# Strided V in two loads a batch, and a new list schedule, in a sparse-attention and gated-projection kernel on one core

## The chip, the core and the metric

The kernel runs on one core of one Trainium2 chip. Its engines work from queues of their own: TensorE (PE, with its weight loads shown apart as PEld), VectorE (DVE), ScalarE (ACT), GpSimd (POOL) and SyncE (SP), which here only issues DMAs. The metric is the device time of one execution, in microseconds (us), lower being better. The span of a profiled execution is the time from its first to its last instruction.

## The reference

Eight batches, eight heads, 576 positions, head size 64. The first four heads see a local window of 32 positions; the other four see the positions with the same residue modulo 32. The attention output then passes a causal convolution of five taps with a sigmoid, and two 512x512 products. All inputs are float32, except that the three weights arrive as float64.

```python
scores = scale * np.matmul(q, k.transpose(0, 1, 3, 2))
mask_local = (rel >= 0) & (rel < stride)
mask_strided = (rel >= 0) & (pos[None, :] % stride == pos[:, None] % stride)
...
attn = np.exp(scores - max) / (sum + 1e-09)
x = np.matmul(attn, v)                 # heads side by side: (8, 576, 512)
...
gate = 1.0 / (1.0 + np.exp(-gate_pre)) # gate_pre: five taps of x
val = x @ w_val
out = gate * val @ w_out
```

## The kernel before, in words

The work of a batch falls into groups, each with a name of a letter, the batch and a number; this text writes L, S, Y, T, V, P and C for the kinds.

- L: scores of the local heads, three groups a batch of 24 matmuls `bank<-KL,qLs`. DVE adds a mask and takes the maximum, POOL subtracts, ACT takes the exponential, POOL scales, DVE transposes. Y: the product with V, two groups a batch of 40 matmuls `bank<-PL,vLs`.
- S: scores of the strided heads, two groups a batch of 32 matmuls `bank<-KBS,qSs`, with the same softmax. T: the product with V, two groups a batch of 16 matmuls `bank<-BDS,vSs`. T reads all 128 partitions of `vSs`.
- C: the convolution of the first of four channel blocks of batch 0 on PE, 10 matmuls `bank<-xs,gate` and `bank<-xs,diag`; all other convolutions are on DVE and ACT (`taps`).
- V and P: the two products by 512x512 weights, in 48 and 36 groups of 12 matmuls. To keep float32 accuracy, the operands are split into a high and a low part (`xhi`, `xlo`, `ghi`, `glo`), and so are the weights (`wv`, `wo`), which are made from float64 at the start, through the buffers `xs`, `osb` and `gate`.
- Filler: matmuls of zeros, `bank<-idle`, that the planner puts into gaps on PE in the first 75 us of its own time, so that PE stays busy. They are fixed in number and place when the program is built; PE runs them whether or not the data that they wait for has come.

One buffer each serves `qLs`, `KL`, `qSs`, `KBS`, `vLs` and `vSs` for all batches, so that the load for a batch can be issued only when the last matmul of the batch before has read it. All loads and stores are issued by SP, in one order, through eight completion semaphores in turn: the ninth DMA is issued when the first has landed, and so on.

The order on every engine comes from `Plan.issue`, a list scheduler that runs when the program is built (lines 133 to 234). It keeps a clock for each engine, and takes of the steps that can start at the earliest time the one whose group has the lowest number in the table `RANK`. Its model of a load is `ISSUE` on SP, then a common pipe that the loads fill one after another for as long as each takes (the `took` that the function `load` sets), then `TO_END` until the data may be read. Its model of PE's program is that it is fetched in blocks of `BLOCK` = 256 words: when PE enters a block, the fetch of the next one starts and takes `FETCH` (more while loads are under way), and PE cannot enter that one before it is there. A matmul of float32 operands counts 4 words, for two passes of a weight load and a matmul; one of bf16 or of the split operands counts 2. The first block begins with 66 words already used.

```python
199                    there = at_edge + self.FETCH + min(2.0, 0.5 * max(0.0, pipe - at_edge))
...
203                free[engine] = start + self.ISSUE
204                pipe = max(pipe, start + self.TO_DATA) + took
205                done = pipe + self.TO_END
```

A row of PE's order is one matmul of this program; the profile counts a float32 one twice (72 rows of L are `x144` there).

Of the kernel before, what the change touches and what calls it, by code (L numbers as in the profile page):

```python
# [19 lines left out]
NT = 18  # L20
# [3 lines left out]
P = 128  # L24
# [9 lines left out]
class Bank:  # L34
# [12 lines left out]
    def now(self):  # L47
        ap = self.hold["tile"]
        for name, a, k in self.chain:
            ap = getattr(ap, name)(*a, **k)  # L50
        return ap
# [6 lines left out]
class Plan:  # L58
# [11 lines left out]
    ENGINES = ("pe", "dve", "act", "pool", "sp")  # L70
    WINDOW, QUIET, BUSY, SLOW = 3.413, 0.48, 0.85, 1.9

    BLOCK, FETCH = 256, 2.4
    ISSUE, TO_DATA, TO_END = 0.6, 1.2, 0.65

    def __init__(self):
        self.filler, self.banks, self.holds = None, None, []
# [160 lines left out]
def tile_sparse_attention_moe(  # L238
# [13 lines left out]
    nc = tc.nc  # L252
# [6 lines left out]
    plan = Plan()  # L259

    def tiles(n, shape, name, dtype=F32, space=None):
        return [(space or pool).tile(shape, dtype, name=f"{name}{i}") for i in range(n)]
# [10 lines left out]
    def size(ap):  # L273
        n = 1
        for _, k in list(now(ap).ap)[1:]:
            n *= k
        return n
# [21 lines left out]
        return (T.matmul, dict(out=out, lhsT=lhsT, rhs=rhs, start=first, stop=last))  # L299

    def load(group, out, in_):
        n = out.ap[0][1] * size(out)
        plan.add("sp", max(n * 4 / 320e3 + (0.25 if group[-1] == "0" or "w" in group else 0.08), 0.45), group, [(nc.sync.dma_start, dict(out=out, in_=in_))])


    ident = pool.tile([P, P], F32, name="ident")
# [12 lines left out]
    vSs = pool.tile([P, 8, 256], F32, name="vSs")  # L319
# [11 lines left out]
    gates = tiles(4, [P, 2 * S], "gate")  # L331
    BDS = Ring(tiles(NB, [P, 16, 4, NT], "BDS"))
    PS = Ring(tiles(1, [P, 32, 32], "PS"))
# [84 lines left out]
    def weight_part(name, src, dst, e, raw, t, u):  # L418
        raw = raw.rearrange("p (c f) -> p c f", c=4).bitcast(U32)
        load("load " + name, raw, src.bitcast(U32)[:, 2 * P * e:2 * P * (e + 1)].rearrange("(c p) f -> p c f", p=P))  # L420
        cols = slice(P * e, P * (e + 1))
        from_f64("make " + name, raw.rearrange("p c (f w) -> p (c f) w", w=2), t, u, dst[0][:, :, cols], dst[1][:, :, cols])
# [30 lines left out]
    def load_qk(b, kind):  # L453
        group = f"load q{kind}{b}"
        if kind == "L":
            load(group, qLs[:, :, :], qL[b])
            load(group, KL[:, :, STRIDE:], kL[b])
            return

        for j in range(2):  # L460
            load(group, qSs[j::2, :2 * S], qS[b, 64 * j:64 * j + 64])
        for j in range(2):
            load(group, KBS[j::2, j, :, :], kS[b, 64 * j:64 * j + 64])

    def load_v(b, kind):
        group = f"load v{kind}{b}"
        if kind == "L":

            for a in range(2):
                for p in range(2):  # L470
                    at = slice(64 * a + 32 * p, 64 * a + 32 * p + 32)
                    load(group, vLs[at, 1 - a:], vL[b].rearrange("(w r) f -> r w f", r=32)[:, 8 * a:9 * a + 9, 2 * D * p:2 * D * p + 2 * D])
        else:
            for g in range(4):
                load(group, vSs[32 * g:32 * g + 32:2], vS[b, g, 0:16])
            for g in range(4):
                load(group, vSs[32 * g + 1:32 * g + 32:16], vS[b, g, 16:NT])

    def attend_local(b):
        xs = xss[b % 2]  # L480
# [200 lines left out]
    for b in range(B):  # L681
        load_qk(b, "L")
        load_v(b, "L")
        load_qk(b, "S")
        load_v(b, "S")
        attend_local(b)
        attend_strided(b)
        if b == 0:

            raw = [osb2.rearrange("p i f -> p (i f)"), raws[2], raws[3], osb2.rearrange("p i f -> p (i f)")]  # L690
            for e in range(4):
                weight_part(f"wo{e}", w_out, wo, e, raw[e], *[gates[2 * i + e % 2][:, S:S + DM] for i in range(2)])
            zero("dve", "zero xs1", xss[1][:, :, 0:PADK])
        gate(b)
        for k in ((3 * b // 2,) if b % 2 == 0 else (3 * (b // 2) + 1, 3 * (b // 2) + 2)):
            value(k)
            project(k)
    names = list(dict.fromkeys(s[2] for s in plan.steps))
    tile_sparse_attention_moe.end = plan.issue(dict(zip(names, RANK)))


NB = 1
NPL = 1
TAKEN = set()
# [4 lines left out]
CONV = {(0, 0)}  # L709
HELD = set()  # L710
RANK = [
# [12 lines left out]
]  # L724


# [39 lines left out]
```

## Time and profile before

| what | value |
|---|---|
| runs | 331.25, 336.93 and 336.55 us, median 336.55 us |
| the profiled execution | 331.2 us, of which the span is 329.4 us |
| busy in the span: DVE | 225.4 us (68%) |
| busy in the span: ACT, POOL | 189.8 us (58%), 180.8 us (55%) |
| the chain that ended last, by engine | PE 82%, DMA 10%, issue 3%, SP's queue 2% |
| `bank<-idle` on PE | 117 recorded, 30.5 us busy |
| read from and written to HBM | 32.79 MB and 9.44 MB |

A row of the timeline gives the start and the length in us, the engine, the line, the operation, the tile written and those read, the shapes, and the number of instructions joined in the row; in brackets stand the idle time of the engine just before and what ended it. "issue" there means that the engine waited for nothing that the profile shows. Nearly all records have line 226, where the planner issues the instruction; line 351 is the filler. The page's lines by time have 40 slices, 8.235 us each.

### The profile page before, as it was taken

The numbers are of one execution on the slowest core, as the hardware profiler recorded it, in microseconds if no ns is written. First come the engines' busy times: TensorE is split into PE (matmuls) and PEld (weight loads), VectorE is DVE, ScalarE is ACT, GpSimd is POOL, SyncE is SP. The second block draws the span as 40 slices with busy tenths as digits, with TensorE's granted clock in tenths as the row PEclk, the third lists the DMA queues.
The fourth block names the chain that finished last, engine by engine and source line by source line (L and its number), as shares of the span: only waits on it lengthen the run. The fifth ranks groups of instructions, "written<-read, shape, count | busy, mean of one in ns | idle before, by whom it ended". The sixth has DMA issues, their size and how long they took to land.

```text
span 329.4 us, 11806 instructions
## 1 busy us (share of the span) xinstructions
PE 311.0 (94%) x5113; PEld 261.2 (79%) x5120; DVE 225.4 (68%) x438; ACT 189.8 (58%) x373; POOL 180.8 (55%) x213
## 2 busy tenths in 40 slices
PE   8986999997999999899999998999999989999995
PEld 3545567787889989688998887988998978999884
DVE  4479399997988989698592288876776951764300
ACT  4036675695578746574753294498369748442421
POOL 9664767978653964674384276556067722502610
PEclk9997699999999999999999999999999998999999
DMA  7999944469314452676302476036202200100022
GB/s 236 252 178 329 271 137 154 148 203 258 107 66 146 149 211 100 207 235 176 105 2 84 142 197 211 2 105 175 73 1 66 103 4 32 66 32 32 34 96 96
DMA packets 27267, 42.98 MB, mean 130 GB/s; under 512 B 3088, under 2 KB 16912, under 8 KB 26640
## 3 DMA queue, kind: packets, MB, share of 16 engines
q1 hardware_dynamic: 27216, 42.24, 42.9%
q8 instruction: 40, 0.66, 0.9%
q14 instruction: 11, 0.09, 0.1%
HBM read 32.79 MB, written 9.44 MB: 128 GB/s over the span
## 4 chain that ended last, share of the span: by engine, by line
PE 82%; DMA 10%; issue 3%; SPq 2%; ACT 0%; DVE 0%
PE bank L226 73%; PE bank L351 9%; DMA qSs<-in_qS_dram 6%; DMA vSs<-in_vS_dram 3%; SPq L226 2%; DMA vLs<-in_vL_dram 1%; ACT osb L226 0%; DVE idle L350 0%; DVE none L354 0%
## 5 line engine op out<-in xcount | busy, mean ns | idle before, releaser
L226 DVE SCALAR_TENSOR_TENSOR taps<-xs,cw,taps 128x576 f32<-128x576 f32 x124 | 100.6, 811 | 14.3 <-ACT taps L226 12.5
L226 PE MATMUL bank<-xhi,wv 128*128 128x384 f32 x384 | 99.7, 340 | 0.0
L226 PE MATMUL bank<-wo,ghi 128*128 128x512 f32 x288 | 90.8, 397 | 0.0
L226 POOL TENSOR_TENSOR glo<-GV,ghi 128x384 fp32r<-128x384 f32 x48 | 48.3, 1013 | 63.4 <-ACT ghi L226 62.1
L226 PEld LDWEIGHTS bank<-xhi,wv 128*128 128x128 f32 x384 | 68.8, 188 | 2.2
L226 PE MATMUL bank<-xlo,wv 128*128 128x384 f32 x192 | 64.5, 336 | 0.0
L226 PEld LDWEIGHTS bank<-wo,ghi 128*128 128x128 f32 x288 | 53.6, 190 | 11.2
L226 POOL TENSOR_TENSOR xlo<-xs,xhi 128x576 fp32r<-128x576 f32 x32 | 46.2, 1451 | 19.9 <-ACT xhi L226 19.8
L226 PE MATMUL bank<-wo,glo 128*128 128x512 f32 x144 | 56.5, 393 | 0.0
L226 DVE SCALAR_TENSOR_TENSOR GV<-gate,bank 128x384 f32<-128x384 f32 x48 | 26.0, 547 | 34.1 <-PE bank L226 18.0
L226 ACT ACTIVATE osb<-bank 128x512 f32<-128x512 f32 x36 | 21.2, 596 | 30.0 <-PE bank L226 24.5
L226 ACT COPY xs<-bank 128x288 f32<-128x288 f32 x64 | 32.0, 548 | 8.3 <-PE bank L226 8.1
L226 ACT CAST ghi<-GV 128x384 fp32r<-128x384 f32 x48 | 24.0, 510 | 21.6 <-DVE GV L226 21.4
L226 PEld LDWEIGHTS bank<-xlo,wv 128*128 128x128 f32 x192 | 36.0, 188 | 0.0
L351 PE MATMUL bank<-idle 128*128 128x512 bf16 x117 | 30.5, 411 | 5.2 <-issue 3.8
L226 ACT ACTIVATE gate<-taps 128x576 f32<-128x576 f32 x31 | 20.4, 658 | 24.7 <-DVE taps L226 24.6
L226 ACT COPY BDS<-PT 32x288 f32<-32x288 f32 x64 | 27.7, 433 | 9.7 <-DVE PT L226 8.9
L226 PEld LDWEIGHTS bank<-wo,glo 128*128 128x128 f32 x144 | 27.2, 189 | 5.9
L226 POOL TENSOR_TENSOR SML<-SML,ST 128x384 f32<-128x384 f32 x24 | 20.3, 845 | 19.0 <-DVE ST L226 18.8
L351 PEld LDWEIGHTS <-idle 128*128 128x128 bf16 x124 | 12.2, 103 | 20.6 <-issue 7.8
L226 DVE TENSOR_REDUCE ST<-SML 128x6 f32<-128x384 f32 (+1 forms) x48 | 26.0, 545 | 0.9 <-ACT SML L226 0.5
L226 PEld LDWEIGHTS bank<-PL,vLs 32*64 32x64 f32 x1280 | 21.9, 143 | 5.8 <-issue 3.4
(69 smaller groups left out, 371.1 us busy)
## 6 DMA issues: line engine op xcount, KB each, us to landing
out_dram<-osb SPq DMA_DIRECT2D x36, 256.0 KB
qSs<-in_qS_dram SPq DMA_DIRECT2D x16, 288.0 KB
qLs<-in_qL_dram SPq DMA_DIRECT2D x8, 576.0 KB
KL<-in_kL_dram SPq DMA_DIRECT2D x8, 576.0 KB
KBS<-in_kS_dram SPq DMA_DIRECT2D x16, 288.0 KB
vSs<-in_vS_dram SPq DMA_DIRECT2D x32, 128.0 KB
vLs<-in_vL_dram SPq DMA_DIRECT2D x16, 160.0 KB
vLs<-in_vL_dram SPq DMA_DIRECT2D x16, 144.0 KB
```

Source lines behind the costliest of these rows:

```text
L226: got = [fn(**{k: now(x) for k, x in kw.items()}) for fn, kw in calls]
L351: plan.filler = lambda at: T.matmul(out=at, lhsT=idle[:, :P], rhs=idle[:, :], start=True, stop=True)
```

## The change

Three things change in the source. The strided V of a batch is loaded by two DMAs, one of 64 partitions (keys 0 to 15 of each of four groups) and one of 8 partitions (keys 16 and 17), where it was four of 16 partitions and four of 2. The planner's numbers change: `FETCH` from 2.4 to 3.0, `TO_END` from 0.65 to 1.2, and what a load adds to its bytes becomes 0.2 for every load, where it was 0.25 for batch 0 and the weights and 0.08 for the rest. And the table `RANK` is another one. No instruction on DVE, ACT or POOL is added or taken away.

```diff
-    BLOCK, FETCH = 256, 2.4
-    ISSUE, TO_DATA, TO_END = 0.6, 1.2, 0.65
+    BLOCK, FETCH = 256, 3.0
+    ISSUE, TO_DATA, TO_END = 0.6, 1.2, 1.2
...
     def load(group, out, in_):
-        n = out.ap[0][1] * size(out)
-        plan.add("sp", max(n * 4 / 320e3 + (0.25 if group[-1] == "0" or "w" in group else 0.08), 0.45), group, [(nc.sync.dma_start, dict(out=out, in_=in_))])
+        n = 1
+        for k in out.shape:
+            n *= k
+        plan.add("sp", max(n * 4 / 320e3 + LOAD, 0.45), group, [(nc.sync.dma_start, dict(out=out, in_=in_))])
...
-            for g in range(4):
-                load(group, vSs[32 * g:32 * g + 32:2], vS[b, g, 0:16])
-            for g in range(4):
-                load(group, vSs[32 * g + 1:32 * g + 32:16], vS[b, g, 16:NT])
+            for rows, keys in ((slice(0, P, 2), slice(0, 16)), (slice(1, P, 16), slice(16, NT))):
+                load(group, vSs[rows].rearrange("r n f -> r (n f)"),
+                     vS[b, :, keys].rearrange("g t n f -> g t (n f)"))
...
+LOAD = 0.2
...
 RANK = [
-    223, 130, 85, 82, 100, 54, 253, 247, 56, 131, 268, 93, 53, 134, 241, 140, 277, 144, 154, 271, 136, 147, 195, 58,
+    84, 243, 209, 155, 196, 173, 29, 32, 256, 79, 135, 208, 6, 194, 267, 25, 234, 221, 158, 21, 42, 145, 232, 11,
...
```

What this does to the order is seen best on SP, whose queue PE waits for. The first place is the start of the program, SP's first rows before. `in_w_val` and `in_w_out` are parts of the two weights, `in_conv_w` the taps.

```order
L226 DMA xs_77<-in_w_val_dram 128x4x256
L226 DMA qSs<-in_qS_dram 64x1152
L226 DMA osb_110<-in_w_out_dram 128x4x256
L226 DMA qLs<-in_qL_dram 128x1152
L226 DMA KL<-in_kL_dram 128x2x576
L226 DMA vSs<-in_vS_dram 16x2048 x2
L226 DMA KBS<-in_kS_dram 64x1152 x2
L226 DMA qSs<-in_qS_dram 64x1152
L226 DMA vSs<-in_vS_dram 16x2048 x2
L226 DMA xs_78<-in_w_val_dram 128x4x256
```

The same rows of SP now:

```order
L226 DMA xs_77<-in_w_val_dram 128x4x256
L226 DMA qSs<-in_qS_dram 64x1152
L226 DMA osb_110<-in_w_out_dram 128x4x256
L226 DMA cw_91<-in_conv_w_dram 128x4x10
L226 DMA qLs<-in_qL_dram 128x1152
L226 DMA KBS<-in_kS_dram 64x1152
L226 DMA KL<-in_kL_dram 128x2x576
L226 DMA KBS<-in_kS_dram 64x1152
L226 DMA xs_78<-in_w_val_dram 128x4x256
L226 DMA qSs<-in_qS_dram 64x1152
```

The taps and half of the strided K now stand ahead of the local K (`KL`), and V of the strided heads has moved behind them.

A little further on SP now stand the local loads of batches 1 and 2 and what lies between them, whose place in the stream the prediction uses:

```order
L226 DMA vSs<-in_vS_dram 64x1x2048
L226 DMA qLs<-in_qL_dram 128x1152
L226 DMA KL<-in_kL_dram 128x2x576
L226 DMA xs_78<-in_w_out_dram 128x4x256
L226 DMA qSs<-in_qS_dram 64x1152
L226 DMA KBS<-in_kS_dram 64x1152 x2
L226 DMA vSs<-in_vS_dram 8x1x2048
L226 DMA xs_78<-in_w_out_dram 128x4x256
L226 DMA qSs<-in_qS_dram 64x1152
L226 DMA osb_110<-in_w_out_dram 128x4x256
L226 DMA qLs<-in_qL_dram 128x1152
L226 DMA KL<-in_kL_dram 128x2x576
```

Between the local loads of batch 1 and those of batch 2 stand seven rows, among them the three parts of `w_out` that were still to come. Ahead of the first of these rows stand, besides the ten above, the four loads of `vLs` (32x9x128 twice and 32x10x128 twice) and one more part of `w_val` each into `xs_78` and `xs_77`.

The second place is the loads of the strided heads of batch 3, some 70 us into the run before. SP before:

```order
L226 DMA vLs<-in_vL_dram 32x10x128
L226 DMA qSs<-in_qS_dram 64x1152
L226 DMA KBS<-in_kS_dram 64x1152 x2
L226 DMA qSs<-in_qS_dram 64x1152
L226 DMA vSs<-in_vS_dram 16x2048
L226 DMA qLs<-in_qL_dram 128x1152
L226 DMA KL<-in_kL_dram 128x2x576
L226 DMA vSs<-in_vS_dram 16x2048 x3
L226 DMA vSs<-in_vS_dram 2x2048
```

SP now, at the loads for the same batch:

```order
L226 DMA vLs<-in_vL_dram 32x10x128
L226 DMA vSs<-in_vS_dram 64x1x2048
L226 DMA qSs<-in_qS_dram 64x1152
L226 DMA KBS<-in_kS_dram 64x1152 x2
L226 DMA vSs<-in_vS_dram 8x1x2048
L226 DMA qLs<-in_qL_dram 128x1152
L226 DMA qSs<-in_qS_dram 64x1152
L226 DMA KL<-in_kL_dram 128x2x576
```

Five issues of V around these loads have become two, and one part of Q now stands behind the local Q.

PE has the same matmuls in another order, with 122 fillers where it had 124. Its order up to the first V group, in groups with the number of rows, is:

| | rows of PE's order, up to the first V group |
|---|---|
| before | filler 51, L 72, filler 18, S 64, filler 12, Y 80, filler 8, C 5, L 24, C 5, L 24, T 16, L 24, filler 21, T 16, filler 1, S 64, filler 12, V |
| now | filler 59, L 72, filler 14, S 64, filler 47, L 72, T 16, Y 40, S 64, L 24, T 16, Y 40, L 24, filler 1, C 10, T 16, V |

By then L has 48 rows and T 16 rows more than before; the other kinds have as many.

The rows of PE between the last S group of one batch and the first of the next, which is the time that the loads of `qSs` and `KBS` have, are before at the least: for batch 3 two V groups, a T and an L; for batch 6 (the next shortest) a V group, a Y, an L and a P. Now they are at the least, for batch 4: two P groups, a V, a Y and a T.

22 rows, old and new, of the table RANK are left out of this document.

## The prediction

> **What bounds the kernel now.** I read the page first (busy shares, the 40 slices), then PE's timeline, then the waits and SP's timeline.
>
> ```profile
> PE 311.0 (94%) x5113; PEld 261.2 (79%) x5120; DVE 225.4 (68%) x438; ACT 189.8 (58%) x373; POOL 180.8 (55%) x213
> ...
> GB/s 236 252 178 329 271 137 154 148 203 258 107 66 146 149 211 100 207 235 176 105 2 84 142 197 211 2 105 175 73 1 66 103 4 32 66 32 32 34 96 96
> ...
> q8 instruction: 40, 0.66, 0.9%
> ...
> L351 PE MATMUL bank<-idle 128*128 128x512 bf16 x117 | 30.5, 411 | 5.2 <-issue 3.8 <-DVE none L354 1.2
> ```
>
> PE is the bound: no other engine is above 68%. Of its 311 us, 30.5 us are filler, so 280.5 us are work that this change does not touch, and some 49 us of the 329.4 us span can move. Nearly all of that lies before the first V group:
>
> ```profile
> 1.19 12.76 PE L351 MATMUL bank<-idle 128*128 128x512 bf16 x50 [1.19 <-DVE none L354]
> 13.88 1.72 PE L226 MATMUL bank<-KL,qLs 64*32 64x64 f32 x144
> 15.54 4.06 PE L351 MATMUL bank<-idle 128*128 128x512 bf16 x17
> 19.52 0.29 PE L226 MATMUL bank<-KBS,qSs 128*32 128x36 f32 x9
> 20.83 1.26 PE L226 MATMUL bank<-KBS,qSs 128*32 128x36 f32 x119 [1.02 <-issue]
> 22.02 2.12 PE L351 MATMUL bank<-idle 128*128 128x512 bf16 x8
> 27.58 0.82 PE L351 MATMUL bank<-idle 128*128 128x512 bf16 x3 [3.44 <-issue]
> 28.33 3.28 PE L226 MATMUL bank<-PL,vLs 32*64 32x64 f32 x124
> 31.95 1.33 PE L226 MATMUL bank<-PL,vLs 32*64 32x32 f32 x36 [0.34 <-issue]
> 33.62 3.19 PE L351 MATMUL bank<-idle 128*128 128x512 bf16 x7 [0.34 <-issue]
> ...
> 55.83 0.70 PE L226 MATMUL bank<-xhi,wv 128*128 128x384 f32 x2
> ```
>
> The "issue" gaps are edges of instruction blocks. PE and PEld together have 10,233 instructions in 40 fetched blocks, so about 256 to a block. Counted from the 66 words at the start, word 512 falls in the sixth S row of PE's order, where the gap of 1.02 us stands (after 9 profiled matmuls, two to a row), and word 768 some ten fillers later, where the 3.44 us stand. Word 256 passed in the 23rd L row, at about 14.4; the block behind word 512 came at 20.83, so its fetch took 6.4 us. The next took 20.83 to 27.58, 6.75 us; the third, to the gap at 31.95, 4.4 us.
>
> The rest of the recoverable time is in eight later gaps:
>
> ```profile
> 66.44 0.33 PE L226 MATMUL bank<-KBS,qSs 128*32 128x36 f32 x15 [1.27 <-issue]
> 77.00 1.33 PE L226 MATMUL bank<-KBS,qSs 128*32 128x36 f32 x128 [1.96 <-DMA qSs<-in_qS_dram]
> 138.94 1.33 PE L226 MATMUL bank<-KBS,qSs 128*32 128x36 f32 x128 [1.40 <-DMA qSs<-in_qS_dram]
> 195.63 1.39 PE L226 MATMUL bank<-PL,vLs 32*64 32x64 f32 x78 [0.23 <-DMA vLs<-in_vL_dram]
> 199.35 0.31 PE L226 MATMUL bank<-KL,qLs 64*32 64x64 f32 x7 [1.24 <-issue]
> 224.07 0.46 PE L226 MATMUL bank<-PL,vLs 32*64 32x64 f32 x15 [0.34 <-issue]
> 269.94 0.27 PE L226 MATMUL bank<-PL,vLs 32*64 32x64 f32 x2 [1.00 <-issue]
> 270.39 1.97 PE L226 MATMUL bank<-BDS,vSs 128*64 128x72 f32 x32 [0.18 <-issue]
> ```
>
> They sum to 7.6 us: 3.6 us waits for loads, 4.0 us block edges. Where a block holds little work, PE reaches its end before the next is there.
>
> **The change part by part.** *V in two loads.* SP's rows for four old loads, and the wait that its rows show:
>
> ```profile
> SPq L226 <- DMA KL<-in_kL_dram: 7.0, 4, 2.6
> ...
> 13.08 0.37 SPq L226 DMA_DIRECT2D xs<-in_w_val_dram  x1
> ...
> 51.82 2.50 SPq L226 DMA_DIRECT2D vSs<-in_vS_dram  x4
> ...
> 57.30 2.52 SPq L226 DMA_DIRECT2D vSs<-in_vS_dram  x4
> ```
>
> Eight issues took 5.0 us of SP, about 0.63 us each; two take 1.3 us, 3.7 us a batch less. The bytes are the same, and no PE wait before is for `vSs`, so by itself this is worth nothing on the path. PE's other work hides it; if that cover went, the 3.7 us are what a Q load behind V could gain at one place. On the other side, loads that carry more each leave eight semaphores for more bytes; no row prices that, and I bound it by one issue, 0.6 us. I take 0.
>
> *The later gaps.* Before batch 3's S there are two V groups (2.2 us each), a T and an L (0.7): 6.2 us, and PE waited 1.96 us; before batch 6's a V, a Y (1.4), an L and a P (2.9): 7.2 us, and it waited 1.40. So these loads need 8.2 to 8.6 us from the last reader. The durations of groups are these rows:
>
> ```profile
> 61.85 2.76 PE L226 MATMUL bank<-PL,vLs 32*64 32x64 f32 x160
> ...
> 66.72 1.22 PE L226 MATMUL bank<-BDS,vSs 128*64 128x72 f32 x32
> ...
> 84.83 0.72 PE L226 MATMUL bank<-KL,qLs 64*32 64x64 f32 x48
> 85.48 0.62 PE L226 MATMUL bank<-xhi,wv 128*128 128x384 f32 x2
> ...
> 87.67 0.63 PE L226 MATMUL bank<-wo,ghi 128*128 128x512 f32 x2
> ...
> 90.53 1.22 PE L226 MATMUL bank<-BDS,vSs 128*64 128x72 f32 x32
> ```
>
> (V is 85.48 to 87.67, P 87.67 to 90.53, Y half of 2.76.) The shortest stretch now is two P, a V, a Y and a T, 10.5 us: enough by 2 us. I take the waits for Q as gone. I then walked PE's new order in blocks of 256 words with these durations. After the first V group the shortest blocks before held 1.9, 2.4, 2.7 and 2.8 us of work, and those are the four with gaps; now they hold 3.1, 3.7, 4.1 and 4.1. From the gaps at 224.07 and 269.94 a late fetch takes 2.4+0.34 = 2.8 and 2.7+1.0 = 3.7 us, so at most 0.6 us is left. T at 270.39 also ran in 1.97 instead of 1.22 us, the granted clock being below 1 there: 0.75.
>
> ```profile
> 260.00:280.00 20.00, 18.82 (x285) 16.50 (x284) 9.12 (x15) 12.74 (x25) 6.37 (x8) 0.91 0.11 41
> ```
>
> For new waits that I can't see (SP's order puts stores of P ahead of some loads) I take another 0.6 us, bounds 0 and 3. Together −7.6 −0.75 +1.2 = −7.2 us, bounds −8.4 and −4.8.
>
> *Work moved ahead of the first V.* Two L groups and a T that before came later: 2×0.7+1.2 = 2.6 us off the rest.
>
> *The start.* 59 fillers take 12.76 + 9×0.22 = 14.8, to 15.95. Local K lands about then: behind 2.84 MB, against 2.52 MB before, when SP, which waits there for the semaphore of that load, went on at 13.08. At the slices' 252 GB/s that is 1.3 us later, 14.4. (The memset of `vSs` on POOL, now in the middle of the mask, is covered by these fillers.) L 1.72 and 14 fillers (3.3) bring 21.0. Word 256 now passes at 16.3, its fetch comes 6.4 later at 22.7, and word 512 in the fourth S row is a gap of 1.6. S ends at 24.1, word 768 is the sixth of 47 fillers, at 25.4, and the fetch from 22.7 ends at 29.5 (27.1 by the 4.4 us). The planner lets a fetch run beside fillers, but they stand behind it on PE: 41 are still to run, 9.1 us, to 38.6. Then L, from 38.6 to 40.7; word 1024 at 39.9.
>
> Now come three blocks of 2.7, 1.6 and 2.4 us of work (L, T, Y, S, L, T, all float32). At 4.4, 4.4 and 3.3 us a fetch they end at 44.3, 48.7 and 52.0. The loads allow that: by the slices 10.42 MB are moved at 41.2, and local Q and K of batch 2 end at 11.33 MB, so at 44.5 and, with the 2.5 us that the load at 13.08 took beyond its bytes, at 47.0; they are needed near 49. Left are 36 Y rows (1.25), L, ten C rows (5.7, by the rows below), T and a filler: 9.1, and the first V group starts at 61.
>
> ```profile
> 40.75 2.21 PE L226 MATMUL bank<-xs,gate 128*128 128x288 f32 x8
> ...
> 42.80 0.65 PE L226 MATMUL bank<-xs,diag 128*128 128x288 f32 x2
> ```
>
> With 2.8 us a fetch in these blocks, and the short end of the filler gap, the loads bind instead: L of batch 2 from 47.0, V at about 56. With half a window at half clock it is 64. I take 60 between them, +4.2 us.
>
> **The sum.** 329.4 + 4.2 − 2.6 − 7.2 = 323.8 us of span; the execution took 331.2, 1.8 more, so 325.6 us. The median of the runs, 336.55, is 5.4 above the profiled execution; 325.6 is 1.7% below that execution and 3.3% below the median.
>
> The Trainium skill, "Runtime: NRT & Kernel Launch", "Instruction fetch mechanics", has blocks of 16 KiB or 256 instructions, fetched while the current one runs, and calls the cost of crossing an edge "mostly hidden". The 40 blocks agree; the gaps of 3.44 and 1.02 us at the counted words do not. By that rule the block gaps would be no term, and the sum would go by the second rival.
>
> **The rivals.** *The start runs through* (V at 55 to 56): fetches are short because fewer loads are in flight. 329.4 − 0.3 − 2.6 − 7.2 + 1.8 = 321 us. For it: the 4.4 us fetch at 31.95; against it: two of three were above 6.
>
> *Block counts do not govern the late gaps.* They would reappear, 4.0 us: 329.6 us. For it: the profile says only "issue". Against it: the four shortest blocks are the four with gaps. The page of the skill named above stands for this one.
>
> *The start is lost.* The gap at 25.4 halves the clock, as before:
>
> ```profile
> 20.00:40.00 20.00, 15.00 (x307) 10.09 (x309) 13.74 (x32) 11.40 (x26) 11.11 (x12) 0.74 1.11 269
> ```
>
> A mean of 0.74 is about 10 us at half clock; there 7 fillers took 3.19 instead of 1.55 and Y 4.6 instead of 2.76. In the new order up to 24 fillers would lie in those 10 us, +5 us: 331 to 334 us.
>
> *Slower.* The same gap, but the waits at the three short blocks never leave PE a busy stretch, so that it stays at half clock to the first V: 41 fillers at 0.43 (+8.5) and 17 us of groups at 1.5 times (+8.5), V at 73 where the walk without waits has 56: +17. 329.4 + 17 − 2.6 − 7.2 + 1.8 = 338.4 us, just over 2% above the profiled execution. It decides if the clock is half beyond about 60 us. Against it: before it came back within 10 us. That the edit does nothing is no case; the orders differ everywhere.
>
> **How the numbers follow.** The forecast, 323 to 328 us, 0.38; the start runs through, 0.20; late gaps stay, 0.17; the start is lost, 0.17; slower, 0.08. The range 318 to 333 holds all but the fast end of the second, the upper half of the fourth and the last. Two per cent, about what a measurement of this kernel can tell from no change, is at 324.6 us against the profiled execution and at 329.8 against the median. Counting 0.20, six tenths of 0.38 and a little of the third: faster 0.46; same 0.46; slower 0.08.
>
> **What would show it.** Right: no wait of an S group for `qSs` over 0.5 us; no "issue" gap over 0.6 us after 65 us; a gap of 2 to 4 us among the third run of fillers, and the first V group between 56 and 64. Wrong: late waits for `KL` or `vLs` behind a store on SP, gaps in long blocks, or a granted clock below 0.9 in slices after 65 us.

## The result

The changed kernel takes 352.81 us (median of four runs, 351.7 to 356.94) where the kernel before takes 334.08 (four runs, 331.25 to 336.93; the fourth, 331.6, was not yet among those ahead of the prediction): the ratio is 1.067, 95% interval 1.051 to 1.082. Ratios here compare the means of only those runs of each kernel that lie within 1.5% of its fastest, while medians are of all runs, so that a ratio can differ from the quotient of the medians. The kernel is slower, and the prediction of 325.6 us (318 to 333) with 8 in 100 for slower was wrong. The profiled execution took 353.87 us, its span 352.1.

The page of the changed kernel, the lines that answer to those of before:

```profile
PE 320.2 (91%) x5118; PEld 266.7 (76%) x5118; DVE 227.5 (65%) x438; ACT 189.7 (54%) x373; POOL 182.0 (52%) x213
...
PEclk9998966999599998999789999999999999999999
DMA  7999556129304494247400436414421031002022
...
L353 PE MATMUL bank<-idle 128*128 128x512 bf16 x122 | 31.2, 417 | 4.1 <-issue 2.6
```

The work of each engine is as before. PE is busy for 9 us more, and the granted clock goes with that: in slices of 8.8 us it is below 0.8 from 44 to 62, from 88 to 97 and from 167 to 176 us, where before it was so only from 25 to 41:

```profile
PEclk9997699999999999999999999999999998999999
```

The idle time has grown by some 14 us. The timeline of PE shows where; the rows below, of the changed kernel, are all its gaps over 1 us, and its first V group:

```profile
1.19 14.87 PE L353 MATMUL bank<-idle 128*128 128x512 bf16 x59 [1.19 <-DVE none L356]
22.66 1.29 PE L226 MATMUL bank<-KBS,qSs 128*32 128x36 f32 x123 [1.53 <-issue]
27.77 10.93 PE L353 MATMUL bank<-idle 128*128 128x512 bf16 x42 [2.63 <-issue]
...
43.50 0.60 PE L226 MATMUL bank<-PL,vLs 32*64 32x64 f32 x8 [1.12 <-DVE SML L226]
45.23 1.47 PE L226 MATMUL bank<-PL,vLs 32*64 32x64 f32 x72 [1.13 <-DVE PL L226]
50.15 0.94 PE L226 MATMUL bank<-KBS,qSs 128*32 128x36 f32 x46 [2.00 <-issue]
55.12 1.39 PE L226 MATMUL bank<-PL,vLs 32*64 32x64 f32 x78 [1.23 <-DVE SML L226]
...
67.71 0.62 PE L226 MATMUL bank<-xhi,wv 128*128 128x384 f32 x2
...
91.07 2.19 PE L226 MATMUL bank<-BDS,vSs 128*64 128x72 f32 x32 [5.88 <-DMA vSs<-in_vS_dram]
133.82 0.71 PE L226 MATMUL bank<-KL,qLs 64*32 64x64 f32 x48 [3.24 <-DMA KL<-in_kL_dram]
173.68 2.19 PE L226 MATMUL bank<-BDS,vSs 128*64 128x72 f32 x32 [4.87 <-DMA vSs<-in_vS_dram]
246.14 0.44 PE L226 MATMUL bank<-xhi,wv 128*128 128x384 f32 x1 [1.12 <-issue]
```

The waits for `qSs` and most block gaps of before are gone after 68 us, as forecast, and the gap of 2.63 us among the third run of fillers was forecast too. But three waits of 3 to 6 us for loads have come, two of them for `vSs`, for which PE had no gap before. The T groups behind the two waits for `vSs` run in 2.19 us where 1.22 is usual; from 91.0 to 93.3 us the granted clock is 0.50. And the first V group starts at 67.71, where it started at 55.83 before and was forecast between 56 and 64. The chain of the changed kernel says how long four loads took from their issue to their landing (start, length, what):

```profile
57.45 8.97 DMA vSs<-in_vS_dram
...
78.15 12.79 DMA vSs<-in_vS_dram
...
121.03 12.65 DMA KL<-in_kL_dram
...
163.65 9.94 DMA vSs<-in_vS_dram
```

The load at 78.15 is the one of 8 partitions. Its 64 KB would take 0.5 us at the 122 GB/s that this profile has on average, so its bytes alone do not explain 12.79 us.

### The profile page after: what moved, and what is told of

Same layout as the page of the kernel before. It is cut to its first block, busy times and chain, and to the rows that moved or that the text cites. A ratio compares the mean times of both kernels' runs of the same rounds, so it can differ in the third digit from the quotient of the medians.

```text
span 352.1 us, 11735 instructions
## 1 busy us (share of the span) xinstructions
PE 320.2 (91%) x5118; PEld 266.7 (76%) x5118; DVE 227.5 (65%) x438; ACT 189.7 (54%) x373; POOL 182.0 (52%) x213
## 2 busy tenths in 40 slices
DMA packets 26755, 42.98 MB, mean 122 GB/s; under 512 B 2576, under 2 KB 16400, under 8 KB 26128
## 4 chain that ended last, share of the span: by engine, by line
PE 78%; DMA 13%; DVE 3%; issue 2%; ACT 2%; POOL 1%; SPq 1%; ACTq 0%
PE bank L226 69%; DMA vSs<-in_vS_dram 9%; PE bank L353 9%; DMA KL<-in_kL_dram 4%; DVE gate L226 2%; SPq L226 1%; DVE ST L226 1%; ACT BDS L226 1%; POOL wv L226 0%; DVE SML L226 0%; ACT osb L226 0%; ACT xs L226 0%; POOL SML L226 0%; POOL PB L226 0%; ACT taps L226 0%
## 5 line engine op out<-in xcount | busy, mean ns | idle before, releaser
L226 PE MATMUL bank<-xhi,wv 128*128 128x384 f32 x384 | 104.3, 353 | 1.1 <-issue 1.1
L226 PEld LDWEIGHTS bank<-xhi,wv 128*128 128x128 f32 x384 | 71.5, 196 | 3.5 <-issue 1.4
L226 PE MATMUL bank<-xlo,wv 128*128 128x384 f32 x192 | 66.5, 346 | 0.0
L226 PEld LDWEIGHTS bank<-xlo,wv 128*128 128x128 f32 x192 | 37.5, 195 | 0.0
L226 PE MATMUL bank<-BDS,vSs 128*64 128x72 f32 x512 | 22.0, 245 | 12.0 <-DMA vSs<-in_vS_dram 12.0
L226 PEld LDWEIGHTS bank<-BDS,vSs 128*64 128x64 f32 x512 | 19.7, 151 | 15.6 <-issue 8.5
```

The costliest lines, as they stand in the source:

```text
L226: got = [fn(**{k: now(x) for k, x in kw.items()}) for fn, kw in calls]
```

## The experiments

**Which part costs.** The first four runs cross the two orders with three ways to load V. In all of them the instructions of PE, DVE, ACT and POOL stand in the order of the kernel that is named; only SP's DMAs of `vSs` differ. For eight loads in the new order, one step of the planner issues four DMAs:

```diff
+                def four(out, in_, step=step, keys=keys):
+                    for g in range(4):
+                        nc.sync.dma_start(out=vSs[32 * g + (step > 2):32 * g + 32:step], in_=vS[b, g, keys])
+                load(group, vSs[(step > 2):P:step].rearrange("r n f -> r (n f)"), None, four)
```

> The order of the changed kernel, instruction for instruction on PE, DVE, ACT and POOL, with strided V again in four loads of 16 partitions and four of 2, issued where the two loads stood. Theory A (the merged load runs on few of the DMA engines, because its DRAM side has four groups as its outermost dimension, and holds up what is queued behind it): the waits for vSs (12.0 us) and KL (3.2 us) of the changed kernel go, with some 6 us of half clock behind them: 329 to 336 us, in place of 352.8. Theory B (the new order is what costs, whatever the loads): 345 to 353 us. Theory C (a load that is large as such lands late, and fewer semaphores let more bytes stand in the queue): as A here, 329 to 336.

It took 337.72 us, ratio to before 1.021 (1.013 to 1.029), a little above what theories A and C expected. Waits of 1.18 us for `vSs` and 1.24 for `KL` are left on PE. So 15 us of the loss are the merged loads, and some 5 us stay with the order.

For two loads in the old order, the first of each four steps issues the merged DMA and the other three nothing; the planner's numbers are the old ones.

> The order of the kernel before, instruction for instruction on PE, DVE, ACT and POOL, with strided V in the two merged loads of the change, each issued where the first of its four stood. A: slower than before (334.1 us) by the late V and what queues behind it, 340 to 360 us; vSs waits on PE of several us each. B: 331 to 336 us, as before. C: as A, 340 to 360.

351.9 us, ratio 1.060 (1.049 to 1.072). The merged loads cost at least as much in the order that was made for eight. PE's waits for `vSs` are fewer than expected there, 3.12 and 1.17 us; beside them stand 4.0 us for `KL` and 5.1 for `qSs`.

In the next two the host lays V out so that the rows of each load lie in one piece:

```diff
-            for rows, keys in ((slice(0, P, 2), slice(0, 16)), (slice(1, P, 16), slice(16, NT))):
-                load(group, vSs[rows].rearrange("r n f -> r (n f)"),
-                     vS[b, :, keys].rearrange("g t n f -> g t (n f)"))
+            for rows, keys in ((slice(0, P, 2), slice(0, 64)), (slice(1, P, 16), slice(64, 72))):
+                load(group, vSs[rows].rearrange("r n f -> r (n f)"), vS[b, keys])
```

> The order of the changed kernel with its two loads, but with V laid out by the host so that the 64 rows of the one and the 8 rows of the other each lie in one piece in DRAM: the DRAM side's outermost dimension is 64 or 8 where it was 4. Same number of loads, same bytes, same places on SP. A: as with eight loads or a little better, 327 to 336 us, no wait for vSs above 1 us. B: 345 to 353. C: 345 to 353, with the waits for vSs still there. The Trainium skill, DMA: Bandwidth & Descriptors, section on why a DMA increments its semaphore by 16, says that the number of engines is the largest up to 16 that divides the outermost dimension of both sides, so 4 for the merged loads and 16 and 8 here; that is theory A.

332.71 us, ratio 1.005 (0.997 to 1.013). PE has no wait for `vSs`. After the first V group its timeline has one gap over 0.2 us:

```profile
224.73 0.44 PE L226 MATMUL bank<-xhi,wv 128*128 128x384 f32 x1 [0.89 <-issue]
```

It is the one at 246.14 in the changed kernel, behind the same matmul of the same V group.

> The order of the kernel before with the two flat loads of the run ahead of this one. A: as before or a little less, 328 to 336 us, since SP has fewer issues and the bytes land as they did. B: 331 to 336. C: 340 to 360.

330.67 us, ratio 0.998 (0.990 to 1.007).

| | eight loads | two, four pieces in DRAM | two, one piece each |
|---|---|---|---|
| old order | 332.58 us | 351.9 us | 330.67 us |
| new order | 337.72 us | 352.81 us | 332.71 us |

(The 332.58 is the kernel before in the runs beside these.) Same bytes, same number of loads and same places on SP, and yet about 20 us between the last two columns: theory C, that a load is late because it is large, falls, and so does B as the main cause. What differs is the outermost dimension of the DRAM side, 4 in one and 64 or 8 in the other. With flat loads the two orders differ by 2 us, and the intervals of their ratios overlap.

**How many engines.** The trace has a count for that. The page's line on DMA packets gives those under 512 B, and their number changes from kernel to kernel only with the loads of V. First the kernel before, then the changed one, then the new order with flat loads:

```profile
DMA packets 27267, 42.98 MB, mean 130 GB/s; under 512 B 3088, under 2 KB 16912, under 8 KB 26640
```
```profile
DMA packets 26755, 42.98 MB, mean 122 GB/s; under 512 B 2576, under 2 KB 16400, under 8 KB 26128
```
```profile
DMA packets 26883, 42.98 MB, mean 130 GB/s; under 512 B 2704, under 2 KB 16528, under 8 KB 26256
```

If a load leaves one small packet on each DMA engine that it uses, eight batches leave 8×(4×16+4×2) = 576 before, 8×(4+4) = 64 with the change and 8×(16+8) = 192 with flat loads. Taking these off gives 2512 in all three. That fits if the old large loads used 16 engines and the old small ones 2, and each merged load 4; the next two runs had their counts forecast by it. The Trainium skill, "DMA: Bandwidth & Descriptors", section "Why a DMA increments its semaphore by 16 and not by 1", has this rule: of at most 16 engines a DMA uses the largest number that divides the outermost dimension (sizes of 1 left out) of both its sides, and it uses the lowest-numbered. The traces agree with the number, by these counts and by those of the next two runs; which engines they are, no run here shows.

Two runs change only the layout of V in DRAM, to 8 or to 2 pieces, each with its share of both loads. Beside the line below, the slices and the host's layout change with the number of pieces (not shown):

```diff
-                load(group, vSs[rows].rearrange("r n f -> r (n f)"), vS[b, keys])
+                load(group, vSs[rows].rearrange("r n f -> r (n f)"), vS[b, :, keys])
```

> As the new order with two flat loads, but V lies in DRAM in 8 pieces, each of 8 rows of the one load and 1 row of the other, so that the outermost dimension of the DRAM side is 8 for both. Theory A: 8 engines a load, the large load takes about half as long as with 4: 333 to 340 us, and 8 x (8+8) = 128 packets under 512 B for the ends of these loads, so 2640 in the page's line. Theory C (size only): 345 to 353.

341.1 us, ratio 1.041 (1.030 to 1.052), just above what was expected, with the 2640 packets under 512 B that were forecast.

> As the run ahead of this one with V in 2 pieces, of 32 and 4 rows. Theory A: 2 engines a load, each with 262 KB: twice as slow as with 4, waits for vSs of 10 us and more at most batches, 385 to 430 us; 8 x (2+2) = 32 packets, so 2544 under 512 B. Theory C: 345 to 353.

379.48 us in one run, a little under what was expected, with the 2544 packets forecast. The waits of PE in that run (total, number, longest) are under 10 us each:

```profile
PE bank L226 <- DMA vSs<-in_vS_dram: 27.9, 5, 9.0
PE bank L226 <- DMA KL<-in_kL_dram: 5.6, 1, 5.6
```

So one order with two loads takes 332.7, 341.1, 352.8 and 379.5 us with 16, 8, 4 and 2 engines for the large load. With 8, no wait of PE for `vSs` is left in the profile:

```profile
30.48 12.04 PE L353 MATMUL bank<-idle 128*128 128x512 bf16 x42 [4.00 <-issue]
...
158.53 0.27 PE L226 MATMUL bank<-PL,vLs 32*64 32x64 f32 x2 [2.02 <-issue]
```

What is longer there than with 16 is mostly the start (the first V group at 70.97 against 67.56, behind a block gap of 4.00 us where the other has 2.35), the block gap of 2.02 us at 158.53 and a wait for DVE of 1.09 us. Why blocks come later there was not tried.

The trace also records, outside the views shown here, the time of every increment of the semaphore that tells that a load has landed. For the large load of batch 3 and the part of Q issued right behind it (times in us; a single increment about 1 us after the issue, where there are fewer than 16, is left out):

| run | issue of the large load | its increments | the last of them | after the issue | increments of the Q load behind it |
|---|---|---|---|---|---|
| one piece | 75.45 | 16 | 79.16 | 3.7 | 16 by 80.89 |
| 8 pieces | 78.86 | 8 | 86.52 | 7.7 | 8 by 85.32, 8 by 87.11 |
| 4 pieces (the changed kernel) | 75.62 | 4 | 87.93 | 12.3 | 12 by 81.05, 4 by 88.34 |
| 2 pieces | 84.07 | 2 | 98.59 | 14.5 | 14 by 88.21, 2 by 99.28 |

The large load has as many increments as it has engines by the count of packets, and takes longer the fewer they are, though not in proportion: with 2 it does not take twice as long as with 4, as theory A expected. The load behind it is late on just as many of its sixteen.

**Which of the two loads.** The longest wait ended on the small load. Two runs make one load flat and leave the other in four pieces, with a row left free between the pieces. The first of them:

```diff
+            for rows, src in ((slice(0, P, 2), vS[b, 0:64]),
+                              (slice(1, P, 16), vS[b, 64:76].rearrange("(g t) f -> g t f", t=3)[:, 0:2])):
+                load(group, vSs[rows].rearrange("r n f -> r (n f)"), src)
```

> The new order with two loads, the large one flat (64 rows in one piece) and only the small one (keys 16 and 17, 8 rows, 64 KB) in 4 pieces in DRAM, with a gap of one row after each. Theory A, by bytes an engine: 2 rows of 8 KB on each of 4 engines is little, so 332 to 336 us, as with both flat (332.7). If the small load is what hurts, since it was the one that a wait of 5.9 us in the changed kernel ended on: 345 to 353.

331.41 us, ratio 1.011 (1.005 to 1.017), in effect as with both loads flat.

> The same with the large load in 4 pieces and the small one flat. Theory A: 16 rows of 8 KB, 131 KB, on each of 4 engines: 347 to 354 us, nearly all of the loss of the changed kernel (352.8), with waits for vSs and KL. If the small load is what hurts: 332 to 337.

357.55 us, ratio 1.076 (1.063 to 1.090), above what was expected and 4.7 us above the changed kernel; a block gap of 6.19 us at 32.10, where that kernel has 2.63, is most of the difference. The chain of this run again shows late loads of `vSs` and `KL`:

```profile
62.17 8.55 DMA vSs<-in_vS_dram
...
82.48 13.43 DMA vSs<-in_vS_dram
...
125.20 11.62 DMA KL<-in_kL_dram
```

The large load costs all of it: 0.524 MB on 4 engines are 131 KB each, against 33 KB with 16. The loads behind it land late because a share of each waits on those engines, and there the wait is written down. The semaphore increments show it for batch 3 of this run: the large load's four come at 92.07 to 93.01 us, 13.1 us after its issue, and of the flat small load's eight, four come by 89.07 and four only from 94.75 to 95.91.

**Where the gain of the order went.** With flat loads the new order should have been the kernel that the prediction priced, 325.6 us, and it takes 332.7. Its windows, of 6 and of 10 us (columns: the window, its length, then busy us and instructions of PE, PEld, DVE, ACT and POOL, the granted clock, the DMA share and GB/s):

```profile
34.00:40.00 6.00, 6.00 (x94) 2.93 (x92) 0.46 (x1) 0.00 (x0) 0.00 (x0) 1.00 0.41 137
```
```profile
50.00:60.00 10.00, 8.53 (x256) 7.23 (x256) 10.00 (x20) 5.60 (x12) 7.53 (x7) 0.50 0.69 204
```

and DVE's and PE's timelines at that place:

```profile
40.08 0.62 DVE L226 TENSOR_TENSOR SML<-bank,maskF 128x192 f32<-128x192 f32 x2 [5.61 <-PE bank L226]
```
```profile
23.65 1.29 PE L226 MATMUL bank<-KBS,qSs 128*32 128x36 f32 x123 [2.64 <-issue]
28.47 10.93 PE L353 MATMUL bank<-idle 128*128 128x512 bf16 x42 [2.35 <-issue]
39.33 1.72 PE L226 MATMUL bank<-KL,qLs 64*32 64x64 f32 x144
44.20 0.60 PE L226 MATMUL bank<-PL,vLs 32*64 32x64 f32 x8 [2.00 <-DVE SML L226]
```

Until 39.33 us PE runs fillers, and from 34 to 40 DVE (but for 0.46 us), ACT and POOL stand idle, because the next thing in their queues needs the L groups that stand behind the fillers. Afterwards DVE has the softmax and the making of the weights at once and is full from 50 to 60, PE waits for it three times between 42 and 56 us (2.00, 1.13 and 1.06 us), and the clock is at half from 50 to 60. One run takes most of the third run of fillers away:

```diff
-                    for _ in range(fill):
+                    for _ in range(fill if start < 20.0 else min(fill, 12)):
```

> The new order with the two flat loads, and of the third run of fillers, 47 matmuls ahead of the L groups of batch 1, only 12. Theory D (in the new order PE reaches those L groups late because the fillers stand in its queue behind two block gaps, and DVE, ACT and POOL, which wait for these groups, stand idle until then; that is where the expected gain of the order went): the first L group of batch 1 starts near 30.5 us in place of 39.3, the first V group 6 to 9 us earlier than 67.6, the time 322 to 327 us in place of 332.7. Rival E (the start is bound by loads or by the making of the weights on DVE, and the fillers only fill): 330 to 334 us, with the idle time moved to waits behind DVE or DMA.

325.91 us (ten runs, 324.64 to 327.96). The L groups start at 30.02 and the first V group at 62.01, 9.3 and 5.6 us earlier:

```profile
30.02 1.47 PE L226 MATMUL bank<-KL,qLs 64*32 64x64 f32 x120
...
38.69 0.75 PE L226 MATMUL bank<-PL,vLs 32*64 32x64 f32 x8 [2.33 <-DVE SML L226]
...
62.01 0.62 PE L226 MATMUL bank<-xhi,wv 128*128 128x384 f32 x2
```

That is close to what D expected, the first V group a little short of it. The rest of the 9.3 us is lost again in waits for DVE and for blocks: DVE is busy for 9.46, 9.90 and 10.00 us of the three tens from 30 to 60. So D is right on the fillers, and E on DVE as what binds next; no wait of PE for a load is left in this run.

> The new order, both loads flat, and none of the 47 fillers of the third run (nor the single one after it), where 12 of them gave 325.9 us. Theory D: the first L groups of batch 1 come another 1 to 3 us earlier, until their load binds; the clock may go to half a window sooner: 322 to 328 us. Rival (the fillers keep the clock up and are worth their time): 329 to 335.

325.59 us (four runs, 323.91 to 328.2). Whether 12 of these fillers are left or none makes no difference in time, though without them the granted clock is 0.50 from 30 to 50 us, where it is 0.85 and 0.63 in these two tens with 12.

These two are the lowest medians of all kernels here. The kernel before, beside them, had medians of 331.27 and 332.66 us, with single runs from 326 to 337 us. The ratios are 0.993 (0.989 to 0.997) and 0.983 (0.973 to 0.992), a gain of 0.7 and 1.7%, which is small beside that spread.

## Why the prediction was wrong

- **V in two loads** is the step that failed: "by itself this is worth nothing on the path", with 0.6 us as its bound for a loss. It cost 19 us in the old order (351.9 against 332.58) and 15 in the new (352.81 against 337.72). The step counted bytes and issues, found both equal or better, and took for granted that a load of 64 partitions runs as wide as one of 16. What the runs showed in its place: the merged load ran on 4 engines, landed 12.3 us after its issue in batch 3 where the flat one took 3.7, and held up the loads behind it. The bound was made of an issue on SP, which has nothing to do with how many engines carry the bytes. The form of the DRAM side, four groups of 16 rows with a gap between them, stood in the diff. No rival had it either: the one on the slower side was a clock that stays at half, and half clock came only as a consequence, behind the waits.
- **SP's saved issues** are worth at most 2 us: with flat loads the old order takes 330.67 us, ratio 0.998, which includes no change.
- **The later gaps** were right, for the order: with flat loads one of 0.89 us is left in place of eight, and from the first V group to the end it takes 330.7 − 67.56 = 263.1 us, against 329.4 − 55.83 = 273.6 before. That is 10.5 us less; the prediction's two terms, 7.2 for the gaps and 2.6 for the work moved ahead, made 9.8 (one profiled execution each). (The old order with flat loads takes 328.4 − 53.03 = 275.4.) So the rival that the late gaps come back, with 4.0 us, falls for flat loads.
- **The one gap that is left** stands where the walk's count has a block with over 5 us of work, because the walk counted only matmuls and weight loads. Ahead of it have run 4167 of each, so with the 66 words 8400, which is 48 short of 33 blocks; at the edge of word 512 the same count is 2 short. Between the two the trace records 46 semaphore instructions in PE's queue, which the profile's counts leave out, and they are just the difference: the gap stands on the edge. In the kernel before, the shortfall grows by 42 and 50 from word 512 to the gaps at 199.35 and 224.07, with 42 and 50 semaphore instructions between. The block that ends at this gap holds the end of a Y, an L and an S, about 2 us, and not the 3.1 us that the prediction had as its shortest. The trace has the fetch too, 16 KB from 222.36 us for 0.98 us; PE goes on 1.4 us after it, and before it went on 1.4 to 1.5 us after such a fetch at 20.83, 27.58 and 31.95. So the account of short blocks held, but the walk misplaced the later edges. With other loads the same order had later block gaps again, as the 2.02 us with 8 pieces.
- **The start** was mis-sized: +4.2 us forecast, +11.7 measured with flat loads (67.56 against 55.83). The two block gaps of 1.6 and 4.1 us came as 2.64 and 2.35, and the L groups at 39.33 where the walk had 38.6. From there the walk counted PE, blocks and loads alone. The work of DVE, ACT and POOL, which these engines could not start before, was left out; the waits for DVE and the half clock from 50 to 60 come with it, and what each of them costs was not separated. That is the rival called "the start is lost" in its size, by another mechanism. One reading of the walk was off without effect: its 44.5 us for the loads of batch 2 takes 271 GB/s beyond 41.2 us, where the next slice has 137, which gives 47.8; no wait of PE for a load stands there in the run with flat loads.
- **The total** of the order alone, 332.7 us with flat loads, lies at the upper edge of the range given; the merged loads put the kernel 20 us above it.

## What to carry to other kernels

Before loads are merged, look at the outermost dimension on both sides of the new access pattern, on the DRAM side too: here it cut a load from 16 DMA engines to 4, and the loads queued behind it were late as well. A layout in which the rows of the merged load lie in one piece kept both the few issues and, for the load of 64 rows, the width. And filler matmuls stand in the queue ahead of real work: where the work behind them feeds other engines, count what those engines have to do afterwards before calling the time free.

## What was not expected of the hardware

- The time follows the number of engines of the large V load, with the order and the bytes unchanged: 332.7, 341.1, 352.8 and 379.5 us for 16, 8, 4 and 2. (The small load has 8, 8, 4 and 2 there; on 4 engines alone it cost nothing.)
- The number of engines can be read off a profile, by the count of packets under 512 B: 2512 plus one for each engine of each V load, in all seven ways to load V (3088, 2576, 2704, 2640, 2544, and 2672 and 2608 with one load flat).
- A wait of 5.88 us for a load of 64 KB was not that load's own: its cause was the large load issued ahead of it, which landed 12.3 us after its issue on 4 engines.
